# Last half batch of a fused attention / expert / gate kernel: value products over seven steps, copied by ScalarE, no taps in the last four steps

## The chip, the cores and the metric

The kernel runs on one core of a Trainium2 chip. The core has five engines with one instruction queue each, worked off in order: TensorE (PE; its weight loads are shown as PEld), VectorE (DVE), ScalarE (ACT), GpSimd (POOL) and SyncE (SP), which here only issues DMAs. Engines wait for each other by semaphores. The metric is the device time of one execution in microseconds (us), median of three runs.

## The reference, cut to what matters

Three blocks follow each other: attention with pooled queries, a mixture of four experts that are causal attentions of their own, and a gated dense block. The change lies where the second block ends and the third begins.

```python
# second block, per expert e (4 batches of 576 tokens, 512 channels)
scores = scale * (q @ k.transpose(0, 2, 1))      # causal mask, softmax -> a
ye = a @ v @ wo[e]                               # out += weight of e per token * ye
# third block
gate_pre += conv_w[k][None, None, :] * xp[:, k:k + S, :]   # 5 taps along the tokens
gate = 1.0 / (1.0 + np.exp(-gate_pre))
val = x @ w_val
return (gate * val @ w_out)
```

Since `x` is `a @ v @ wo`, the kernel multiplies `wo` and `w_val` together beforehand (the tile `wf`), and computes `val` for a batch straight from the tiles `y` = `a @ v`.

## The kernel before, in words

Everything is computed in fp32 split into a high and a low part (three products for one). The second block walks 40 steps: batch b (4) x half g (2, two experts each) x query tile i (5, in the order 1, 3, 2, 4, 0), plus two trailing steps (LAG = 2). Step n computes scores (`scores2`, L804 or L811, into one of two PSUM buffers `s`; mask and row extreme on DVE, L813 to L816) and their exponentials on ACT (`expo2`, L825 or L827); it normalises the probabilities of step n-1 (`norm2`: three or four small DVE operations, L834 to L844, then a multiplication on POOL, L840 or L845), and transposes those of step n-2 on PE (`transp2`, L864 or L876), from where `evac` (L850) copies them out of PSUM, in turns by ACT and by DVE (both L852/L854). After the last tile of a half, `av2` multiplies probabilities and values on PE (L891, L904); ACT writes the high part of the result (L224), DVE the low part (L225).

Between these fixed parts a step fills PE with work from a list `fill`: it pops entries until the estimated PE time `t` reaches `budget`, which spreads what is in the list over the steps that are `left` until the next half. Behind each popped entry go the DVE and ACT operations that earlier entries left in `late2`, and one "ride": a tap of the convolution on DVE (L215, `tap`), as long as `room` is not used up. So the order on each engine is the order in which this Python code runs; nothing reorders it later.

At step 35 (n = 10 * B - 5), where the last half of the last batch begins, 14 of 16 "value products" of batches 0 and 1 are put into `fill` (`raws`): `value` (L769) makes 6 matmuls of 288 columns into a PSUM tile `a`, and a copy takes it to the tiles called k, q and v in the rows (`first3["raw"]`). The other two follow behind the last `av2`. PSUM tiles named `a` share four banks: a matmul group that takes a bank waits for the last reader of the tile that had it.

Behind the steps comes the third block: sigmoids of the gates (L785), gate times value on DVE (`gate_all`, L1123), eight `mix` groups on PE (L923, with copies L924 and L925 on ACT and their taps on DVE), `spread` (high part on ACT L780, low part on DVE L781) and 18 output groups `final` on PE (L1107), which need these parts and end the kernel.

Of the kernel before, what the change touches and what calls it, by code (L numbers as in the profile page):

```python
# [12 lines left out]
AF = mybir.ActivationFunctionType  # L13
# [7 lines left out]
def tile_kernel(ctx, tc, q, k, v, w_gate, wq, wk, wv, wo, w_val, conv_w, w_out, wo_t, q0, k0, out):  # L21
# [741 lines left out]
    def value(yhs, b, m, hf, then):  # L763

        qsl = slice(hf * HQ, (hf + 1) * HQ)
        ps = ps_m.tile([P, 512], F32, name="a")
        ops = [(wi, yi, g) for g in range(EP) for wi, yi in THREE]
        for o, (wi, yi, g) in enumerate(ops):
            pe.matmul(ps[:, 0:HQ], lhsT=wf[:, g, wi, m * P:(m + 1) * P], rhs=yhs[b, g][:, yi, qsl], start=o == 0, stop=o == len(ops) - 1)  # L769
        late2.append(lambda: then(ps[:, 0:HQ], m, qsl))  # L770
# [16 lines left out]
    with ExitStack() as s2l:  # L787
# [61 lines left out]
        def evac(dst, src):  # L849
            turn[0] += 1  # L850
            if turn[0] % 2:
                act.activation(dst, src, AF.Copy)  # L852
            else:
                dve.tensor_copy(dst, src)  # L854
# [128 lines left out]
        for n in range(len(steps) + LAG):  # L983
            if n < len(steps):
                b, g, i = s = steps[n]
                if n % 5 == 0:
                    pts[b, g] = (pt_p2.tile([P, 4, 2, SQ], F32, name="pt"), pt_p2.tile([R64, 2, R64], F32, name="pt4"))
                    if g == 0 and b:
                        fill += proj(xh[b], 1, (lambda: xh.update({3: load2(3)})) if b == 2 else None)
                        if b == B - 1:  # L990
                            fill.append((0, lambda: late2.append(begin3)))
                    if n == 10 * B - 5:
                        buf = [f(c2.tile([P, 2, SQ], F32R, name=f"k20{i}")) for i in range(2)]
                        bufs = [c2.tile([P, SQ + R64], F32R, name=f"q20{i}") for i in range(2)]
                        v2 = v_p.tile([P, 5, ED + E], F32, name="v2").rearrange("p t c -> p (t c)")
                        first3["raw"] = [[buf[t // 2][:, t % 2] for t in range(KT)], [f(bufs[t])[:, 0:SQ] if t < 2 else v2[:, (t - 2) * SQ:(t - 1) * SQ] for t in range(KT)]]
                        raws = [(0.74, lambda i=i, m=m, hf=hf: value(yhs, i, m, hf, lambda ps, m, qsl: evac(first3["raw"][i][m][:, qsl], ps))) for i in range(2) for m in range(KT) for hf in range(2)]
                        fill += raws[0:14]
                    if b == 0 and g == 1:
                        buf = y0_p.tile([P, EP, 2, SQ], F32R, name="y0")  # L1000
                        yhs.update({(0, i): buf[:, i] for i in range(EP)})
                    if b == 1 and g == 0:
                        buf = y12_p.tile([P, 2, EP, 2, SQ], F32R, name="y12")
                        yhs.update({(1 + j, i): buf[:, j, i] for j in range(2) for i in range(EP)})
                if n % 10 == 5 and b + 1 < B:
                    fill += proj(xh[b + 1], 0)
                if n % 10 == VG and b + 1 < B:
                    v2s[b + 1], gws[b + 1], vg = vgate(xh[b + 1])
                    fill += vg
                if n == 0:  # L1010
                    fill += proj(xh[0], 1)
                if n == FD:
                    fill += [(2.6, lambda g=g: fold(g)) for g in range(EP)]
            t = 0.0
            left = 5 - n % 5
            own = [ahead(m) for m in range(n, n + left)]
            budget = max(FL, (sum(c for c, _ in fill) + (PEND if 10 <= n and n % 10 < PN else 0) + sum(own)) / left) - own[0]

            room = [3]

            def ride():
                if urgent:
                    urgent.pop(0)()
                    return
                if rides and room[0]:
                    room[0] -= 1
                    rides.pop(0)()

            def pop(rider=True):
                c, a = fill.pop(0)  # L1030
                now, late2[:] = late2[:], []
                a()
                for x in now:
                    x()
                if rider:
                    ride()
                return c

            if 0 <= n - 1 < len(steps):
                norm2(steps[n - 1], gws[steps[n - 1][0]])  # L1040
            for _ in range({0: 1, 5: 3}.get(n, 0)):
                t += pop()
            if n < len(steps):
                scores2(s)
            if fill:
                t += pop(RD[n % 5])
            else:
                flush()
            if n >= LAG:
                b1, g1, i1 = steps[n - LAG]  # L1050
                transp2(steps[n - LAG], pts[b1, g1])
                if i1 == ORDER[-1]:
                    if g1 == 1:
                        then = (lambda b1=b1: fill.extend(mix(b1, [yhs[b1, 0], yhs[b1, 1]]))) if b1 < B - 1 else begin_last
                    else:
                        then = (lambda: None) if b1 < B - 1 else load_wo3
                    fill[IN:IN] = av2(v2s[b1], pts[b1, g1], g1, yhs[b1, g1], then)
            if n < len(steps):
                expo2(s)
            if n == 0:  # L1060
                flush()
            while fill and t < budget:
                t += pop()
            ride()
            if n == 9:
                xh[2] = load2(2)
            if n in (12, 22):
                flush()
            if n % 10 == 9:
                flush()  # L1070
                while urgent:
                    urgent.pop(0)()
# [16 lines left out]
    with ExitStack() as s3:  # L1089
# [33 lines left out]
                dve.tensor_tensor(out=raw, in0=raw, in1=first3["gp"][i][m], op=ALU.mult)  # L1123

        gates3 = [(0, lambda i=i, m=m: spread(first3["raw"][i][m], gs[0], m, i * SQ)) for i in range(2) for m in range(KT)]
        rest = values(2, gp2) + values(3, end3["gp"])
        fin = [[(2.6, lambda i=i, t=t: final(i, t)) for t in range(9)] for i in range(2)]
        mixs = mix(B - 1, [yhs[B - 1, g] for g in range(EP)])
# [5 lines left out]
        for i in range(len(VF)):  # L1134
            if i == 9:
                assert len(rest) <= 8
            todo.append((fin[0] + fin[1])[i])
            if i == 0:
                todo.append((0, lambda: gate_all(1)))
                todo += gates3  # L1140
            if i == 2:
                todo.append((0, lambda: sigm(gp2.values())))
            if i == 6:
                todo.append((0, lambda: sigm(end3["gp"].values())))
            todo += rest[0:VF[i]]
            del rest[0:VF[i]]
# [49 lines left out]
```

## Time and profile before

| what | value |
|---|---|
| median of 3 runs | 764.3 us (763.15 to 764.69) |
| the profiled execution, its own time | 763.82 us |
| its span in the trace | 762.0 us |
| PE busy | 746.6 us, 98% of the span |
| DVE busy | 568.6 us, 75% |
| ACT busy | 448.4 us, 59% |
| POOL busy | 316.3 us, 42% |
| mean granted TensorE clock | 0.998 |

The stretch that the change touches lies at 656 to 714 us of the span. A row of the timeline gives the start, the busy time, the engine, the line, the operation, out<-in with shapes and the number of instructions merged into it; in brackets stands how long the engine had been idle and what released it. A busy time includes the emptying of the engine's pipeline, so the next row of the same engine can start before it ends; the cost of an operation in a row without idling is therefore the distance between two starts.

### The profile page before, as it was taken

What the parts mean: (1) busy time and instruction counts of PE and PEld (TensorE: products, weight loads), DVE (VectorE), ACT (ScalarE), POOL (GpSimd) and SP (SyncE); (2) the same over time, 40 slices, a digit from 0 to 9 for tenths busy, and PEclk for the clock granted to TensorE, in tenths of its full rate; (3) what the DMA queues carried; (4) which work ended last, traced back from release to release, by engine and by line L of the source; (5) the groups of instructions that cost most, each with busy time, mean ns of one, the idle gap of its engine ahead of it and who ended that gap; (6) DMA issues with size and microseconds to landing.
All of it is one profiled execution on the core that took longest, in us unless ns stands there. A gap on an engine that the chain in (4) does not pass through costs nothing.

```text
span 762.0 us, 14765 instructions
## 1 busy us (share of the span) xinstructions
PE 746.6 (98%) x5315; PEld 618.1 (81%) x5315; DVE 568.6 (75%) x1062; ACT 448.4 (59%) x986; POOL 316.3 (42%) x443
## 2 busy tenths in 40 slices
PE   8999999999999999999999999999999999989998
PEld 7787887787788777878878877988899888878887
DVE  5777898898888988756766766355789798978730
ACT  5665675665656656656656756335464655647632
POOL 6564675675676675653543511022322322220000
PEclk9999999999999999999999999999999999999999
DMA  6967778778778698777657581478325753800212
GB/s 248 262 144 211 216 198 253 194 227 251 196 243 258 174 269 230 199 210 212 156 166 224 134 281 58 111 210 194 118 64 140 198 145 88 272 1 15 83 57 96
DMA packets 83785, 133.52 MB, mean 175 GB/s; under 512 B 19072, under 2 KB 55424, under 8 KB 83712
## 3 DMA queue, kind: packets, MB, share of 16 engines
q1 hardware_dynamic: 83712, 132.58, 61.2%
q8 instruction: 42, 0.69, 0.4%
q14 instruction: 31, 0.25, 0.1%
HBM read 53.37 MB, written 21.76 MB: 99 GB/s over the span
## 4 chain that ended last, share of the span: by engine, by line
PE 88%; DVE 7%; ACT 2%; DMA 1%; issue 1%; SPq 0%; POOLq 0%; DVEq 0%; ACTq 0%
PE s L440 21%; PE t L489 19%; PE t L519 18%; PE a L242 7%; PE o L1107 7%; PE a L275 4%; PE a L904 3%; PE s L804 2%; PE a L769 2%; DVE gp L215 2%; PE a L876 2%; PE t L478 1%; DVE nm L814 1%; PE a L760 1%; DMA pt<-in_k_dram 1%
## 5 line engine op out<-in xcount | busy, mean ns | idle before, releaser
L452 ACT ACTIVATE p<-s,nm 128x1152 f32<-128x1152 f32 x144 | 176.1, 1223 | 87.1 <-DVE nm L445 84.8
L445 DVE TENSOR_REDUCE nm<-s 128x1 f32<-128x1152 f32 x144 | 192.2, 1352 | 15.6 <-PE s L440 15.3
L489 PE MATMUL t<-ident,p 128*128 128x128 f32 x1296 | 199.0, 275 | 0.8 <-DVE xf L521 0.3
L489 PEld LDWEIGHTS t<-ident,p 128*128 128x128 f32 x1296 | 149.1, 141 | 26.7 <-ACT pt L497 7.0
L497 ACT ACTIVATE pt<-t 128x384 f32<-128x384 f32 x224 | 102.4, 489 | 81.4 <-PE t L489 76.1
L519 PE MATMUL t<-pt,vn 128*64 128x256 f32 (+1 forms) x1152 | 146.8, 408 | 0.0
L499 DVE COPY pt<-t 128x384 f32<-128x384 f32 x208 | 110.3, 554 | 44.8 <-PE t L489 40.9
L519 PEld LDWEIGHTS t<-pt,vn 128*64 128x64 f32 x1152 | 80.1, 137 | 55.8 <-issue 5.3
L440 PE MATMUL s<-ka,qst 128*128 128x384 f32 x384 | 115.8, 383 | 1.7 <-ACT ka L576 1.0
L440 PE MATMUL s<-kb,qst 128*128 128x384 f32 x384 | 99.0, 367 | 0.0
L840 POOL TENSOR_TENSOR p<-p,sm 128x512 f32<-128x512 f32 (+3 forms) x32 | 40.1, 1254 | 106.2 <-DVE sm L838 71.3
L440 PEld LDWEIGHTS s<-kb,qst 128*128 128x128 f32 x384 | 60.8, 189 | 13.6 <-issue 13.1
L440 PEld LDWEIGHTS s<-ka,qst 128*128 128x128 f32 x384 | 63.7, 192 | 3.2 <-ACT ka L576 1.7
L377 POOL TENSOR_TENSOR hlk<-kt,hlk 128x384 fp32r<-128x384 f32 x45 | 45.5, 1011 | 1.1
L521 DVE TENSOR_TENSOR xf<-t,rb 128x320 f32<-128x320 f32 (+1 forms) x32 | 14.6, 457 | 41.4 <-PE t L519 40.8
L242 PE MATMUL a<-xh,wqk 128*128 128x288 f32 x288 | 43.2, 300 | 2.1 <-DVE pt L854 2.1
L825 ACT ACTIVATE p<-s,nm 128x256 f32<-128x256 f32 (+3 forms) x64 | 33.0, 523 | 20.1 <-DVE nm L814 20.1
L467 POOL COPY rm<-rs 128x256 f32<-128x256 f32 x31 | 12.4, 399 | 77.3 <-DVE rs L462 71.2
L528 POOL CAST xt<-xf 128x320 fp32r<-128x320 f32 (+1 forms) x32 | 13.6, 426 | 71.5 <-DVE xf L521 70.9
L215 DVE SCALAR_TENSOR_TENSOR gp<-x,cw,gp 128x572 f32<-128x572 f32 (+3 forms) x48 | 40.7, 850 | 2.6 <-ACT gp L925 2.1
L242 PEld LDWEIGHTS a<-xh,wqk 128*128 128x128 f32 x288 | 39.4, 188 | 3.4 <-DVE pt L854 2.5
L440 PE MATMUL s<-hlk,mixed 128*128 128x384 f32 x135 | 33.7, 357 | 0.0
(190 smaller groups left out, 1170.6 us busy)
## 6 DMA issues: line engine op xcount, KB each, us to landing
ka<-hlk SPq DMA_DIRECT2D x90, 192.0 KB, 3.2
kb<-hlk SPq DMA_DIRECT2D x90, 192.0 KB, 3.6
vn<-in_v_dram SPq DMA_DIRECT2D x16, 576.0 KB, 7.3
k<-hl SPq DMA_DIRECT2D x32, 288.0 KB, 4.9
kt<-in_k_dram SPq DMA_DIRECT2D x15, 576.0 KB, 6.2
qt<-in_q_dram SPq DMA_DIRECT2D x15, 576.0 KB, 5.5
qst<-hlq SPq DMA_DIRECT2D x60, 128.0 KB, 3.3
xh<-x_d SPq DMA_DIRECT2D x12, 576.0 KB, 6.0
```

Of the source, the lines that this page charges most:

```text
L215: dve.scalar_tensor_tensor(out=gp[:, n:], in0=x[:, 0:SQ - n], scalar=cw[:, m, c:c + 1], in1=gp[:, n:], op0=ALU.mult, op1=ALU.add)
L242: pe.matmul(ps[:, 0:HQ], lhsT=wqk[wi][:, t, cs], rhs=xh[t][xi][:, qsl], start=o == 0, stop=o == len(ops) - 1)
L377: late.append(lambda: pool.tensor_tensor(out=hlk[:, 1, gs], in0=kt[:, gs], in1=f(hlk[:, 0, gs]), op=ALU.subtract))
L440: pe.matmul(ps[:, 0:GW], lhsT=ops[c][0], rhs=ops[c][1], start=c == 0, stop=c == len(ops) - 1)
L445: dve.tensor_reduce(d["nm"], d["s"][:, :, 0:GW], axis=AX.XY, op=ALU.min)
L452: act.activation(d["p"], d["s"][:, :, 0:GW], AF.Exp, bias=d["nm"], scale=-1.0, accum_out=sums[(2 * n + u) % len(sums)][:, i:i + 1])
L489: pe.transpose(ps[:, j * P:(j + 1) * P], p[:, g, j * P:(j + 1) * P], ident)
L497: act.activation(dst, src, AF.Copy)
L499: dve.tensor_copy(dst, src)
L519: pe.matmul(ps[64 * h:64 * h + 64, 0:N], lhsT=vn[:, h, j, :], rhs=pt[:, j, h, :], start=j == 0, stop=j == C - 1)
L840: pool.tensor_tensor(out=pv, in0=pv, in1=sm[:, :, None].to_broadcast([P, 2, w]), op=ALU.mult)
L1107: pe.matmul(ps[:, 0:w], lhsT=hl[xi][:, kt, t * P - a:(t + 1) * P - a], rhs=end3["wo3"][:, kt, wi, c:c + w], start=o == 0, stop=o == len(op ...
```

## The change

Three edits, all of them for the last half batch (n >= 35). The copies of the 16 value products are made by ACT alone instead of in turns by ACT and DVE. The budget spreads the list over the steps that are left including the two trailing ones (seven, where it was five), and without the lower bound FL. And `room`, the number of taps that may ride in a step, falls from 3 to 2 at n = 36 and 37 and to 0 from n = 38 on. Two assertions about taps that are left over are added; they make no instruction.

```diff
-                        raws = [(0.74, lambda i=i, m=m, hf=hf: value(yhs, i, m, hf, lambda ps, m, qsl: evac(first3["raw"][i][m][:, qsl], ps))) for i in range(2) for m in range(KT) for hf in range(2)]
+                        raws = [(0.74, lambda i=i, m=m, hf=hf: value(yhs, i, m, hf, lambda ps, m, qsl: act.activation(first3["raw"][i][m][:, qsl], ps, AF.Copy))) for i in range(2) for m in range(KT) for hf in range(2)]
...
-            left = 5 - n % 5
+            left = 5 - n % 5 if n < 35 else len(steps) + LAG - n
             own = [ahead(m) for m in range(n, n + left)]
-            budget = max(FL, (sum(c for c, _ in fill) + (PEND if 10 <= n and n % 10 < PN else 0) + sum(own)) / left) - own[0]
-
-            room = [3]
+            budget = max(FL if n < 35 else 0, (sum(c for c, _ in fill) + (PEND if 10 <= n and n % 10 < PN else 0) + sum(own)) / left) - own[0]
+
+            room = [0 if n > 37 else 2 if n > 35 else 3]
...
+        def check_rides(b):
+            assert not rides if b == B - 1 else len(rides) <= KT * (KC - 1)
+
```

What this does to the order shows at three places. First PE, behind the `av2` of half 0 of the last batch. A name with a number is one tile: `a_...` a PSUM tile of the four banks, `s_...` one of the two score buffers, `p_...` probabilities. Before, the six matmuls of a value product stand between any two fixed parts:

```order
L769 MATMUL a_8715<-y0_6687,wf_6461 128x288 x5
L876 MATMUL a_8730<-ident_62,p_8593 128x128 [waits Activation_49,Pool_49]
L876 MATMUL a_8730<-ident_62,p_8593 128x128 x3
L769 MATMUL a_8738<-y0_6687,wf_6461 128x288 [waits DVE_49,PE_49]
L769 MATMUL a_8738<-y0_6687,wf_6461 128x288 x5
L769 MATMUL a_8747<-y12_7002,wf_6461 128x288 [waits Activation_49]
L769 MATMUL a_8747<-y12_7002,wf_6461 128x288 x5
L811 MATMUL s_8760<-k210_6177,q210_6173 128x288 x2
```

and now, at the same place:

```order
L811 MATMUL s_8712<-k210_6177,q210_6173 128x288 x2
L811 MATMUL s_8712<-k211_6178,q211_6174 128x288 [waits DMAHW5_49,DMAHW0_49]
L811 MATMUL s_8712<-k211_6178,q211_6174 128x288
L811 MATMUL s_8712<-k210_6177,q210_6173 128x288 x2
L811 MATMUL s_8712<-k211_6178,q211_6174 128x288 x2
L769 MATMUL a_8727<-y0_6687,wf_6461 128x288 [waits Activation_49]
L769 MATMUL a_8727<-y0_6687,wf_6461 128x288 x5
L876 MATMUL a_8741<-ident_62,p_8636 128x128 [waits Activation_49,Pool_49]
L876 MATMUL a_8741<-ident_62,p_8636 128x128 x3
L876 MATMUL a_8747<-ident_62,p_8636 128x128 [waits DVE_49]
L876 MATMUL a_8747<-ident_62,p_8636 128x128 x3
L769 MATMUL a_8754<-y0_6687,wf_6461 128x288 [waits DVE_49]
```

In front of these L811 rows PE had made nine value products before and has made four now; the others stand later, up to the second `av2`. The transposes into a_8747 take the bank of a_8681, the first `av2` tile, whose last reader is DVE.

Second DVE at the same place. Before, the low parts of the `av2` result (L225 on hl_8430) stand in front of the small operations of the next step:

```order
L814 TENSOR_REDUCE nm_8706<-s_8705 128x2 [waits DVE_49]
L225 SCALAR_TENSOR_TENSOR hl_8430<-a_8682,hl_8430 128x128 [waits DMAHW2_49,DMAHW1_49,DMAHW7_49,DMAHW0_49,Activation_49]
L225 SCALAR_TENSOR_TENSOR hl_8430<-a_8686,hl_8430 128x448 [waits Activation_49]
L215 SCALAR_TENSOR_TENSOR gp_8559<-x2_8558,cw_97,gp_8559 128x572 [waits DMAHW6_49]
L854 COPY k201_8582<-a_8715 128x288 [waits PE_49]
L215 SCALAR_TENSOR_TENSOR gp_8559<-x2_8558,cw_97,gp_8559 128x573 [waits DVE_49]
L215 SCALAR_TENSOR_TENSOR gp_8559<-x2_8558,cw_97,gp_8559 128x574 [waits DVE_49]
L834 TENSOR_SCALAR sm_8707<-sm_8707 128x2 [waits Activation_49,Pool_49]
```

and now behind them:

```order
L814 TENSOR_REDUCE nm_8672<-s_8671 128x2 [waits DVE_49]
L215 SCALAR_TENSOR_TENSOR gp_8525<-x2_8524,cw_97,gp_8525 128x575
L215 SCALAR_TENSOR_TENSOR gp_8559<-x2_8558,cw_97,gp_8559 128x572 [waits DMAHW6_49]
L834 TENSOR_SCALAR sm_8673<-sm_8673 128x2 [waits Activation_49,Pool_49]
L835 RECIPROCAL sm_8673<-sm_8673 128x2 [waits DVE_49]
L838 TENSOR_TENSOR sm_8673<-sm_8673,gw_7940 128x2 [waits DVE_49]
L813 TENSOR_TENSOR s_8712<-s_8712,cmask2_78 128x64 [waits PE_49]
L814 TENSOR_REDUCE nm_8713<-s_8712 128x2 [waits DVE_49]
L816 TENSOR_TENSOR nm_8713<-nm_8713 128x1 [waits DVE_49]
L225 SCALAR_TENSOR_TENSOR hl_8430<-a_8681,hl_8430 128x128 [waits DMAHW2_49,DMAHW7_49,DMAHW1_49,DMAHW0_49]
L225 SCALAR_TENSOR_TENSOR hl_8430<-a_8685,hl_8430 128x448
```

The low parts moved behind the six operations of sm_8673 and s_8712; the first of these waits for ACT's exponentials p_8674.

Third DVE behind the last `av2`, at the start of the third block. Before:

```order
L225 SCALAR_TENSOR_TENSOR hl_8431<-a_8879,hl_8431 128x448 [waits Activation_49]
L1123 TENSOR_TENSOR k200_8581<-k200_8581,xh_8432 128x576 [waits Activation_49] x2
L1123 TENSOR_TENSOR k201_8582<-k201_8582,xh_8432 128x576 [waits Activation_49] x2
L854 COPY v2_8585<-a_8921 128x288 [waits PE_49]
L781 TENSOR_TENSOR wqk1_8442<-k200_8581,wqk0_8441 128x512 [waits Activation_49]
```

and now:

```order
L225 SCALAR_TENSOR_TENSOR hl_8431<-a_8876,hl_8431 128x448 [waits Activation_49]
L215 SCALAR_TENSOR_TENSOR gp_8559<-x2_8558,cw_97,gp_8559 128x573
L215 SCALAR_TENSOR_TENSOR gp_8559<-x2_8558,cw_97,gp_8559 128x574 [waits DVE_49]
L1123 TENSOR_TENSOR k200_8581<-k200_8581,xh_8432 128x576 [waits Activation_49] x2
L1123 TENSOR_TENSOR k201_8582<-k201_8582,xh_8432 128x576 [waits Activation_49] x2
L215 SCALAR_TENSOR_TENSOR gp_8559<-x2_8558,cw_97,gp_8559 128x575 [waits DVE_49]
L781 TENSOR_TENSOR wqk1_8442<-k200_8581,wqk0_8441 128x512 [waits Activation_49]
```

Three taps that had been done in the steps stand here now, and one copy is gone.

## Rows read from the trace of the kernel before

**Rows 1.** Timeline of PE, last half batch: start us, us, engine, line, operation

```profile
661.15 1.06 PE L769 MATMUL a<-y,wf 128*128 128x288 f32 x6 [1.08 <-DVE pt L854]
...
665.74 0.44 PE L891 MATMUL a<-pt,v 128*64 128x128 f32 x4 [0.80 <-DVE pt L854]
666.01 2.80 PE L904 MATMUL a<-pt,v 128*64 128x448 f32 x20
668.74 0.97 PE L804 MATMUL s<-k,q 128*128 128x384 f32 x4
...
671.51 1.83 PE L769 MATMUL a<-y,wf 128*128 128x288 f32 x12 [0.58 <-DVE hl L225]
673.18 1.22 PE L811 MATMUL s<-k,q 128*128 128x288 f32 x8
674.23 0.96 PE L769 MATMUL a<-y,wf 128*128 128x288 f32 x6
675.03 1.04 PE L876 MATMUL a<-ident,p 128*128 128x128 f32 x8
...
682.42 0.44 PE L876 MATMUL a<-ident,p 128*128 128x128 f32 x2 [0.47 <-POOL p L840]
683.47 0.44 PE L891 MATMUL a<-pt,v 128*64 128x128 f32 x4 [0.61 <-DVE pt L854]
```

**Rows 2.** Timeline of DVE in the same stretch

```profile
661.01 0.45 DVE L854 COPY k<-a 128x288 f32<-128x288 f32 x1
661.38 1.54 DVE L215 SCALAR_TENSOR_TENSOR gp<-x,cw,gp 128x575 f32<-128x575 f32 x2
662.83 0.46 DVE L854 COPY k<-a 128x288 f32<-128x288 f32 x1
663.19 0.16 DVE L834 TENSOR_SCALAR sm<-sm 128x2 f32<-128x2 f32 x1
...
665.27 0.41 DVE L854 COPY pt<-a 128x256 f32<-128x256 f32 x1
...
674.48 0.16 DVE L834 TENSOR_SCALAR sm<-sm 128x2 f32<-128x2 f32 x1
...
676.61 0.45 DVE L854 COPY q<-a 128x288 f32<-128x288 f32 x1
```

**Rows 3.** Timeline of ACT behind the first `av2`

```profile
668.85 0.55 ACT L224 ACTIVATE hl<-a 128x448 fp32r<-128x448 f32 x1 [1.47 <-PE a L904]
671.02 0.60 ACT L852 ACTIVATE pt<-a 128x512 f32<-128x512 f32 x1 [1.62 <-PE a L876]
671.51 0.57 ACT L825 ACTIVATE p<-s,nm 128x384 f32<-128x384 f32 x1
...
672.62 0.42 ACT L852 ACTIVATE k<-a 128x288 f32<-128x288 f32 x1
```

**Rows 4.** Timeline of DVE from the last `av2` to the fifth output group

```profile
687.16 0.62 DVE L225 SCALAR_TENSOR_TENSOR hl<-a,hl 128x448 fp32r<-128x448 f32 x1 [2.61 <-ACT hl L224]
688.58 2.76 DVE L1123 TENSOR_TENSOR k<-k,xh 128x576 f32<-128x576 f32 x4 [0.80 <-ACT xh L785]
...
691.63 0.68 DVE L781 TENSOR_TENSOR wqk<-k,wqk 128x512 fp32r<-128x512 f32 x1
...
712.18 0.42 DVE L781 TENSOR_TENSOR wvg<-v,wvg 128x64 fp32r<-128x64 f32 x2
```

**Rows 5.** Timeline of PE, the fifth output group

```profile
709.52 3.43 PE L1107 MATMUL o<-pt,wvg 128*128 128x512 f32 x12
```

**Rows 6.** Busy time by stretch: length, then PE, PEld, DVE, ACT, POOL, granted clock, DMA

```profile
6.00:9.00 3.00, 1.38 (x5) 0.52 (x4) 1.64 (x2) 1.41 (x4) 0.87 (x1) 1.00 1.04 391
9.00:13.00 4.00, 4.00 (x17) 4.00 (x18) 3.13 (x3) 2.94 (x6) 3.37 (x5) 0.57 1.04 414
...
680.70:684.10 3.40, 2.32 (x20) 1.65 (x20) 1.94 (x7) 1.26 (x6) 0.61 (x1) 1.00 0.00 0
...
696.00:713.00 17.00, 16.98 (x82) 13.64 (x81) 16.79 (x34) 12.24 (x31) 0.00 (x0) 1.00 0.16 62
```

More of the change, by code (lines that the diff above doesn't have):

```diff
@@ L1141, in tile_kernel @@
             if i == 2:
+                todo.append((0, lambda: check_rides(2)))
                 todo.append((0, lambda: sigm(gp2.values())))
             if i == 6:
+                todo.append((0, lambda: check_rides(3)))
                 todo.append((0, lambda: sigm(end3["gp"].values())))
```

## Prediction

> **What bounds the kernel now.** The reading begins with the timeline of PE, since PE is busy nearly all the time and no gap elsewhere can be worth much. In the last half batch the changed stretch, from 656 us to the second `av2` at 683.5, holds its gaps. The four longest are 1.08, 0.80, 0.58 and 0.61 us, and the row behind each names DVE: twice the copy of transposed probabilities, once the low part of the `av2` result, once a copy again [rows 1]. All gaps up to the second `av2` come to about 4 us, with three of 0.25 to 0.5. So 4 us is the most that a better order can bring here. The timeline of DVE shows why PE waits: at 661.0 to 665.7 DVE has no gap, and the copy that PE needs (665.27) is queued behind two value copies, two taps and six operations of the softmax [rows 2]. Then comes the tail. From 696 to 713 both are full, PE 16.98 and DVE 16.79 of 17.00 us [rows 6], and there DVE is the one that decides: the fifth output group takes 3.43 us on PE [rows 5] and ends just behind the last low part that it needs, which DVE begins at 712.18 [rows 4]. Behind that PE runs without a wait to the end. So the end of the kernel moves with DVE's time of arrival at 712, and two things have to be worked out: when the second `av2` comes, and how much more DVE does behind it.
>
> **The copies, part one.** Eight of the 16 copies leave DVE. A copy costs DVE 0.37 us (from 661.01 to 661.38, and 0.36 at the next) [rows 2]; ACT pays about as much, 0.42 us of busy time [rows 3], and has the room. On the path to the first `av2` stand two of them. DVE starts the same taps at 661.0 instead of 661.38, leaves out the second copy, and finishes the probabilities' copy 0.37 + 0.36 = 0.73 earlier, at 664.95 in place of 665.68. The first `av2` needs it, so it starts at 665.0 (665.74 before [rows 1]).
>
> **The spreading.** PE gets there early. Value products are 0.80 us each (674.23 to 675.03 [rows 1]), and only four stand ahead of the first `av2`, where it was six; the scores of the next tile (0.97 us at most) are pulled ahead of it instead. By its own work PE is done at about 663.0: it waits for the copy of the probabilities that ended before 661.15 [rows 1], as before, then does two transposes, one value product and these scores. So it idles 2.0 us where it had idled 0.80. The 0.73 us is gained nevertheless, since DVE sets this time.
>
> **The low part, moved behind a softmax.** The first `av2` takes 3.0 us (665.74 to 668.74 [rows 1]) and ends at 668.05. ACT then makes the high part, one value copy, a copy of four transposed blocks and the exponentials of tile 3. By the distances of [rows 3] that is 0.45 us for the high part, 0.3 for the copy and 0.49 (671.02 to 671.51) for the blocks, so the exponentials begin at 669.35 (PE's transposes are done by then); they take 1.11 us (671.51 to 672.62), and 0.1 until the sum has landed. DVE can start its chain L834 to L816 at 670.6. By then it is through with what the order puts in front (two taps, the chain of tile 3 and its row extremes, two more taps: about 4.8 us from 664.95) and idles. The chain takes 676.61 - 674.48 = 2.13 us [rows 2], and only then comes the low part of `av2`: 672.75 to 673.05. PE meanwhile does four transposes (0.52, half of the row at 675.03), the scores of tile 4 (1.05, 673.18 to 674.23), a value product (0.80) and four more transposes (0.52) [rows 1]: from 668.05 that is 670.95. The next transposes want the bank that DVE has yet to read. So PE idles from 670.95 to 673.1, that is 2.1 us, and this stall takes the place of the one of 0.58.
>
> **From there to the second `av2`.** Nine value products 7.2 us, four and six transposes 0.52 and 0.8, the scores of tile 0 about 0.4 (half of what 384 columns cost is an upper end), five transposes 0.65, and 1.05 from the last transposes to the `av2` (682.42 to 683.47, the wait for the copy included) [rows 1]: 10.6 us. ACT's copies keep ahead of PE here, at 0.3 to 0.42 us each against 0.80 for a product. The narrowest place, by the same walk along the order, is DVE's copy of tile 3's blocks, done about 0.1 us before PE asks for its bank. So the second `av2` starts at 683.7 where it was 683.47: 0.25 us later, though DVE has less to do. If a value product behind a wait costs 0.83 us, as the pair from 671.51 to 673.18 did [rows 1], it is 0.5 later; with a little less ACT time at 669, 0.2 earlier.
>
> **The taps.** `room` 0 leaves three taps of the last channel tile for the tail. DVE runs two of them behind the low part of the second `av2`, in front of the gate products, and the third in the place where the last value copy stood. Before: low part at 687.16, 0.80 us idle, gate products from 688.58, one copy, first low part of `spread` at 691.63 [rows 4]. After: low part at 687.41, taps from 687.95 (0.62 less the overlap), two dependent taps 1.58, so gate products from 689.5 for 2.7, then a tap of 0.73 (half of 661.38 to 662.83 [rows 2]): 692.95. That is 1.3 us later than before, of which 0.25 came with the `av2`; the idle 0.80 us hid part of the three taps. DVE is without a gap from there to 712 [rows 6], so the fifth output group ends 1.3 us later. ACT starts its part of the tail 0.25 + 0.3 later (one more copy), which is less than that and hidden, and PE's eight `mix` groups follow ACT.
>
> **Sum.** -0.73 at the first `av2`, +1.0 in the new wait behind it, +1.05 from the taps: +1.3 us. The profiled execution took 763.8, so 765.1 on its scale; the median of the three runs is 764.3, 0.5 above, so **765.6 us**. Bounds from the places named: second `av2` from 0.2 earlier to 0.5 later, tail 0.8 to 1.4, and 0.3 for the level of a median: 764.7 to 766.6.
>
> **The rivals.** *TensorE's clock falls.* Two gaps of 2 us are longer than any in this stretch so far. The granted clock was 1.00 throughout, also in a stretch in which PE was busy 2.32 of 3.40 us; but at the very start, where PE was busy 1.38 of 3.00 us, the clock of the next 4 us was 0.57, mostly at the lower level of 1.2 GHz [rows 6]. A stretch around either new gap has PE busy for about 1.0 to 1.4 of 3 us, as little as that. One fall costs what the start shows: 0.43 of 4 us, 1.7 us, in matmuls that are on the path (`av2` after the first gap, value products after the second). One gives 767.3, two 769. The Trainium skill (TensorE: Matmul & The Clock Gate, "HAM oscillation — how this bites in real kernels") tells of a clock that falls to half while matmuls wait for transfers, in every turn of a loop, and advises against long idle gaps; its waits are longer than the gaps here, so by its example the clock would hold and the sum would stay at 765.6. The start of this trace speaks against leaning on that: the clock fell there behind waits that were no longer than these.
>
> *DVE's relief pays, not slower.* DVE loses 8 x 0.37 + 3 x 0.73 = 5.2 us of work in a stretch where PE waits for little but DVE. If the exponentials of tile 3 come early enough that the low part is out of the way when PE asks for the bank, the 2.1 us gap goes and the time is 763.5; if the gap before the first `av2` went too, 761.5. It decides itself at the start of DVE's chain L834: it would have to start by 668.5 in place of 670.6. Against it speaks that ACT has the exponentials behind the end of `av2` in its queue.
>
> *The taps are hidden.* If the tail has a wait of DVE's that I don't see, only the 0.25 us stay: 764.6. Against it: 16.79 of 17.00 us [rows 6].
>
> *The edit doesn't do what it says:* it does by the order of instructions, apart from evenness: four products before the first `av2`, ten before the second, four of those in a row.
>
> **How the numbers follow.** A measurement of this kernel can tell about 0.2%, 1.5 us, from no change: 762.8 to 765.8. Forecast 0.42 (0.24 of it below 765.8, 0.18 above); clock 0.27, all slower; DVE's relief 0.2, half of it faster; taps hidden 0.11, no change. So faster 0.10, the same 0.45, slower 0.45. The range reaches into the relief case to 763.0 and over one fall of the clock to 768.0; what is left out is the stronger relief (0.12) and two falls (0.07).
>
> **What would show it.** In the profile of the changed kernel: PE idle for some 2 us ahead of L891 near 665, released by a DVE copy, and for some 2 us near 671 to 673 ahead of L876, released by DVE's L225; DVE idle just before the chain L834 near 670; no PE gap over 0.3 us from there to the second `av2`; three taps around L1123; the output group at 709 stretched by more than the 0.5 us that 3.43 has over its neighbours. Wrong would be: no gap ahead of L876 (the low part comes in time), gaps behind value products that wait for ACT (the copies are late), or a granted clock under 1.00 between 660 and 680.

## The result, and the profile after

The changed kernel takes **769.41 us** (median of six runs, 767.97 to 772.53) against 764.36 (763.15 to 764.69, six runs beside it). The ratio is 1.0070, with a 95% interval of 1.0058 to 1.0082: 5.05 us slower, above the upper end of the forecast range (768.0) and 3.8 us above the forecast.

The mean granted clocks of these six runs lie between 0.991 and 0.998 (before: 0.997 to 1.000); the two runs with 0.998 take 768.6 and 769.1, so the mean clock alone doesn't order the runs.

The profiled execution of after is the slowest of the six: 772.53 us, of which its span is 770.4. Its span is 8.4 us longer than that of before, but 3.5 of these lie ahead of the change: the score group L804 that the changed stretch follows stands at 659.62 and stood at 656.08, and the instructions up to there are the same. So all readings below are distances from that group. Three rows of PE's timeline of before that were not shown yet, the group itself and two output groups (columns: start us, us, engine, line, operation, tiles, shapes, count):

```profile
656.08 0.63 PE L804 MATMUL s<-k,q 128*128 128x256 f32 x4
...
695.98 11.31 PE L1107 MATMUL o<-pt,wqk 128*128 128x512 f32 x48
...
713.58 2.93 PE L1107 MATMUL o<-pt,wvg 128*128 128x512 f32 x12
```

The timeline of PE of after, the rows that answer to these and to [rows 1]:

```profile
659.62 0.63 PE L804 MATMUL s<-k,q 128*128 128x256 f32 x4
...
668.63 0.49 PE L891 MATMUL a<-pt,v 128*64 128x128 f32 x4 [1.94 <-DVE pt L854]
668.88 4.52 PE L904 MATMUL a<-pt,v 128*64 128x448 f32 x20
...
678.83 0.86 PE L876 MATMUL a<-ident,p 128*128 128x128 f32 x4 [2.56 <-DVE hl L225]
679.36 1.81 PE L769 MATMUL a<-y,wf 128*128 128x288 f32 x6
...
690.70 0.44 PE L891 MATMUL a<-pt,v 128*64 128x128 f32 x4 [0.61 <-DVE pt L854]
...
703.51 2.72 PE L1107 MATMUL o<-pt,wqk 128*128 128x512 f32 x11
...
721.86 2.51 PE L1107 MATMUL o<-pt,wvg 128*128 128x512 f32 x10
```

Both gaps of the forecast are there, at the line and with the releaser that it named: 1.94 us ahead of the first `av2`, 2.56 ahead of L876. What the forecast's sum did not have is the length of the work behind them. The same 20 matmuls of L904 take 4.52 us where they took 2.80 [rows 1], and six of L769 take 1.81 where such a group took about 1.0. The granted clock says why. Busy time by stretch of after (length, then PE, PEld, DVE, ACT, POOL, granted clock, DMA share, GB/s):

```profile
614.00:618.00 4.00, 4.00 (x19) 3.95 (x20) 2.75 (x5) 1.59 (x6) 0.00 (x0) 0.57 0.00 1
...
665.00:668.00 3.00, 1.70 (x12) 1.38 (x10) 2.90 (x7) 0.03 (x1) 1.04 (x1) 1.00 0.00 0
...
669.00:672.00 3.00, 3.00 (x12) 1.21 (x10) 2.86 (x8) 1.20 (x5) 1.30 (x1) 0.50 0.00 0
...
675.00:679.00 4.00, 1.44 (x13) 1.20 (x12) 2.50 (x8) 0.90 (x4) 1.47 (x1) 1.00 0.99 335
679.00:682.50 3.50, 3.50 (x17) 3.44 (x17) 2.04 (x8) 1.92 (x5) 0.55 (x1) 0.52 0.53 193
```

Behind each gap the clock is at its lower level, 1.2 GHz: 0.50 from 669 to 672 and, nearly all the time, 0.52 from 679 to 682.5. The prediction had named a clock under 1.00 here as a sign that it would be wrong. In the stretches before, PE was busy 1.70 of 3.00 and 1.44 of 4.00 us. A third fall, at 614 to 618, lies ahead of the change, in work that before has too; it is part of the 3.5 us that this execution brings with it.

The timeline of DVE of after: the wait ahead of the softmax chain, the low part behind it, and the tail that answers to [rows 4].

```profile
676.36 0.17 DVE L834 TENSOR_SCALAR sm<-sm 128x2 f32<-128x2 f32 x1 [2.42 <-ACT p L825]
...
678.50 0.81 DVE L225 SCALAR_TENSOR_TENSOR hl<-a,hl 128x128 fp32r<-128x128 f32 x2
...
694.93 1.66 DVE L215 SCALAR_TENSOR_TENSOR gp<-x,cw,gp 128x573 f32<-128x573 f32 x2
...
699.18 0.81 DVE L215 SCALAR_TENSOR_TENSOR gp<-x,cw,gp 128x575 f32<-128x575 f32 x1
699.91 0.69 DVE L781 TENSOR_TENSOR wqk<-k,wqk 128x512 fp32r<-128x512 f32 x1
```

DVE waits 2.42 us for the exponentials with the low part queued behind the chain, as forecast (the wait is longer than in e9_busy_first below, 0.63, since here the exponentials come behind an `av2` at half clock). The three taps stand in the tail where they were expected.

### The profile page after: what moved, and what is told of

It reads as the page before. It is cut to its first block, busy times and chain, and to the rows that moved or that the text cites. A ratio compares the mean times of both kernels' runs of the same rounds, so it can differ in the third digit from the quotient of the medians.

```text
span 770.4 us, 14766 instructions
## 1 busy us (share of the span) xinstructions
PE 752.7 (98%) x5315; PEld 622.5 (81%) x5315; DVE 566.7 (74%) x1054; ACT 451.0 (59%) x994; POOL 316.9 (41%) x443
## 4 chain that ended last, share of the span: by engine, by line
PE 85%; DVE 8%; DMA 4%; ACT 2%; issue 1%; SPq 0%; DVEq 0%; ACTq 0%
PE s L440 21%; PE t L489 19%; PE t L519 18%; PE a L242 6%; PE o L1107 5%; PE a L275 4%; PE a L904 3%; PE a L769 2%; PE s L804 2%; DVE pt L215 2%; DVE gp L215 1%; PE a L876 1%; DMA k<-hl 1%; PE t L478 1%; DMA xh<-x_d 1%; ACT p L825 1%
## 5 line engine op out<-in xcount | busy, mean ns | idle before, releaser
L224 ACT ACTIVATE hl<-a 128x288 fp32r<-128x288 f32 (+2 forms) x36 | 14.7, 411 | 32.5 <-PE a L242 23.7
```

## The experiments

All kernels have the same instructions up to the score group at 656 us, so one table compares them: for each profiled execution where that group stands, then the distances to the first `av2` (L891), to the second, to the first output group (695.98 in before), to the output group at 713.58 in before, and to the end of the span. "Falls" counts stretches at half clock between that group and the end. The last two columns are over all runs: the median, and the mean of the granted clock (one fall lowers a run's mean by about 0.002; one at the very start, as in [rows 6], counts too, and the profiled execution of before has 0.998 with it).

| kernel | group at | first `av2` | second | output 1 | output 3 | end | sum | falls | median | clock |
|---|---|---|---|---|---|---|---|---|---|---|
| before | 656.08 | 9.66 | 17.74 | 12.51 | 17.60 | 48.4 | 105.9 | 0 | 764.3 | 0.9987 |
| after | 659.62 | 9.01 | 22.06 | 12.81 | 18.35 | 48.5 | 110.8 | 2 | 769.4 | 0.9948 |
| e1_busy | 656.43 | 10.13 | 19.44 | 12.81 | 18.35 | 48.5 | 109.3 | 0 | 768.8 | 0.9973 |
| e2_act_only | 656.37 | 9.25 | 17.03 | 12.81 | 17.58 | 48.5 | 105.2 | 0 | 763.9 | 0.9988 |
| e3_spread_only | 656.38 | 9.28 | 20.98 | 12.51 | 17.60 | 48.5 | 108.8 | 1 | 767.0 | 0.9954 |
| e4_room_only | 655.98 | 9.64 | 17.25 | 12.50 | 19.03 | 48.5 | 106.9 | 0 | 765.7 | 0.9983 |
| e5_low_early | 656.70 | 9.01 | 16.97 | 12.81 | 18.35 | 48.5 | 105.6 | 0 | 765.4 | 0.9978 |
| e6_busy_tight | 657.00 | 8.93 | 19.11 | 12.82 | 18.35 | 48.5 | 107.7 | 0 | 766.8 | 0.9997 |
| e7_act_but_last | 657.35 | 9.26 | 17.02 | 12.51 | 17.59 | 48.5 | 104.9 | 0 | 763.8 | 0.9991 |
| e8_mended | 656.30 | 8.92 | 18.84 | 12.51 | 17.61 | 48.5 | 106.3 | 0 | 764.8 | 0.9990 |
| e9_busy_first | 656.94 | 8.94 | 20.50 | 12.81 | 18.37 | 48.5 | 109.1 | 1 | 767.5 | 0.9980 |
| e10_no_room | 657.48 | 9.02 | 20.33 | 12.81 | 17.60 | 48.5 | 108.3 | 1 | 768.3 | 0.9952 |
| e11_low_first | 655.95 | 9.26 | 16.53 | 12.52 | 17.61 | 48.5 | 104.4 | 0 | 762.6 | 0.9992 |
| e12_low_tap | 657.97 | 8.53 | 16.53 | 12.50 | 17.60 | 48.5 | 103.7 | 0 | 762.2 | 0.9983 |

The theory to test: the change costs a little by its order and tail, and the rest is TensorE's clock, which falls behind two PE gaps that part two makes. The rival: the order costs it all, and the clock is only an onlooker.

**e1_busy: something to do in the gaps.** Matmuls of the identity with itself go into a bank that is overwritten next, 14 ahead of the first `av2` and 14 ahead of the transposes of L876.

```
+ if then is load_wo3:
+     for _ in range(14):
+         pe.matmul(box[0][:, 0:P], lhsT=ident, rhs=ident, start=True, stop=True)
...
+ if s == (B - 1, 1, 3) and e0 == 0:
+     for _ in range(14):
+         pe.matmul(ps[:, 0:P], lhsT=ident, rhs=ident, start=True, stop=True)
```

> The changed kernel with 14 matmuls of 128 columns that nobody reads put into each of the two places where TensorE sits idle for about 2 us (into the first av2 tile ahead of L891, and into the bank of tile 3's first transposes ahead of L876). They keep TensorE at work while it would wait, and lengthen no wait that counts by more than 0.3 us. Theory A (the order costs 1.3 us, and each idle time of about 2 us lets the granted clock fall, at 1.7 us a fall): no fall at 1.2 GHz between 655 us and the second av2, time 765.5 to 766.5. Theory B (the clock is beside the point, the new waits themselves or a later start of the last stretch cost the 5 us): time stays at 769 to 770.

768.81 us (767.06 to 770.02), ratio 1.0059 (1.0042 to 1.0077): by the number, close to theory B. The trace tells another story. No stretch behind the gaps is at half clock, and yet the way from the group to the end is 3.4 us longer than before. The timeline of PE of e1_busy:

```profile
663.35 3.29 PE L894 MATMUL a<-ident 128*128 128x128 f32 x28
666.56 0.44 PE L897 MATMUL a<-pt,v 128*64 128x128 f32 x4
```

The 14 matmuls take 3.29 us, more than the gap that they fill, and delay the first `av2` to 10.13 us behind the group, where after has 9.01; the expectation had allowed for 0.3. Three of the six runs have a mean clock of 0.995 or 0.996 and take 769.8 to 770.0, three have 0.998 or 1.0 and take 767.1 to 767.8. The experiment added a cost of its own and could not decide; e6 mends it.

**e2, e3, e4: the three parts alone.** e2_act_only has part one, the copies on ScalarE:

```
- evac(first3["raw"][i][m][:, qsl], ps)
+ act.activation(first3["raw"][i][m][:, qsl], ps, AF.Copy)
```

> The kernel before with the first edit alone: the 16 value copies on ScalarE, order of PE as before, five steps, room 3. Theory A: the waits of TensorE for VectorE shrink (the 0.80 us ahead of the first av2 by two copies of 0.37 us), the tail on VectorE is one copy shorter, no long idle time, no fall of the clock: 762.5 to 764.0. Theory B (ScalarE's queue is what is late): 765 or more.

763.92 us (762.38 to 765.14), ratio 0.9995 (0.9985 to 1.0004). In the profile the second `av2` comes 1.1 us earlier, of which 0.30 is lost ahead of the first output group and some 0.35 outside the span (last section). The median alone is not told apart from before.

e3_spread_only has part two, the spreading:

```
- left = 5 - n % 5
+ left = 5 - n % 5 if n < 35 else len(steps) + LAG - n
...
- budget = max(FL, (sum(c for c, _ in fill) + (PEND if 10 <= n and n % 10 < PN else 0) + sum(own)) / left) - own[0]
+ budget = max(FL if n < 35 else 0, (sum(c for c, _ in fill) + (PEND if 10 <= n and n % 10 < PN else 0) + sum(own)) / left) - own[0]
```

> The kernel before with the second edit alone: budget over seven steps without the lower bound, copies in turns, room 3. Theory A: the two idle times of about 2 us are made by this edit, so it has them without the others, VectorE is even later ahead of the first av2 (two copies more), and the clock falls once or twice: 766.5 to 770. Theory B (spreading is harmless, the copies or the taps cost the time): 763.5 to 765.

766.98 us (765.73 to 770.74), ratio 1.0038 (1.0023 to 1.0054): the part that costs. PE of e3_spread_only:

```profile
665.66 0.44 PE L891 MATMUL a<-pt,v 128*64 128x128 f32 x4 [2.21 <-DVE pt L854]
665.93 4.23 PE L904 MATMUL a<-pt,v 128*64 128x448 f32 x20
...
675.23 0.66 PE L876 MATMUL a<-ident,p 128*128 128x128 f32 x4 [2.04 <-DVE hl L225]
...
681.03 1.06 PE L769 MATMUL a<-y,wf 128*128 128x288 f32 x6 [0.68 <-DVE pt L854]
```

The two gaps belong to part two; the third, 0.68, is one that part one takes away, since there a DVE copy stands in the queue. Behind the gap of 2.21 the clock fell (L904 takes 4.23), behind that of 2.04 it did not, though PE was no busier around it than in the stretches of after that lost the clock, 1.19 of 3.00 us:

```profile
672.00:675.00 3.00, 1.19 (x10) 0.95 (x8) 2.10 (x7) 0.66 (x4) 1.47 (x1) 1.00 0.97 349
675.00:679.00 4.00, 3.77 (x30) 3.66 (x31) 3.96 (x8) 1.87 (x5) 0.00 (x0) 1.00 0.61 228
```

So a gap of 2 us can bring a fall and need not.

e4_room_only has part three, fewer taps in the last steps:

```
- room = [3]
+ room = [0 if n > 37 else 2 if n > 35 else 3]
```

> The kernel before with the third edit alone: taps in the last steps fewer, the rest of them in the tail. Theory A: VectorE's part behind the second av2 is about 1.4 us longer (three taps of 0.73 less the 0.80 us of idle time), the waits before it are up to 1 us shorter, no idle time near 2 us, no fall of the clock: 764.4 to 765.8. Theory B (the taps cost most of the 5 us): 768 or more.

765.71 us (764.23 to 766.78), ratio 1.0018 (1.0008 to 1.0027), as expected of the taps. Without part two PE gains 0.5 us up to the second `av2` and then stands for the low parts in the tail, PE of e4_room_only:

```profile
699.16 8.86 PE L1107 MATMUL o<-pt,wqk 128*128 128x512 f32 x37 [1.06 <-DVE wqk L781]
```

**e6_busy_tight: the same with sized fillings**, 8 matmuls in the first gap and 10 in the second (the diff of e1_busy with `range(8)` and `range(10)`).

> The whole change, with matmuls that nobody reads in PE's two gaps, as in e1_busy but sized to the gaps: 8 ahead of the first av2 and 10 ahead of L876, at 0.235 us each by e1_busy (3.29 us for 14), 1.9 and 2.35 us. Theory (the time of the change is an order cost of about 0.9 at the second av2 and 1.05 in the tail, and the rest is clock): 764.3 + 1.95 = 766.3, within 765.9 to 766.9, and a mean clock of 0.998 or more. Rival (the clock has little part in it, and the 768.8 of e1_busy is the order): 767.8 to 769.

766.83 us (765.00 to 768.14, 7 runs), ratio 1.0032 (1.0019 to 1.0045); six of the seven runs have a mean clock of 1.000, the seventh 0.998. The timeline of PE, and the stretches of e6_busy_tight that answer to those of after:

```profile
663.92 1.95 PE L894 MATMUL a<-ident 128*128 128x128 f32 x16
665.93 0.44 PE L897 MATMUL a<-pt,v 128*64 128x128 f32 x4
666.20 2.80 PE L910 MATMUL a<-pt,v 128*64 128x448 f32 x20
...
671.28 2.39 PE L876 MATMUL a<-ident 128*128 128x128 f32 x20
...
674.43 0.66 PE L879 MATMUL a<-ident,p 128*128 128x128 f32 x4 [0.33 <-DVE hl L225]
...
685.03 0.44 PE L897 MATMUL a<-pt,v 128*64 128x128 f32 x4 [0.61 <-DVE pt L854]
```

```profile
669.00:672.00 3.00, 3.00 (x25) 3.00 (x26) 2.37 (x4) 2.46 (x7) 0.99 (x1) 1.00 0.62 167
672.00:675.00 3.00, 2.67 (x24) 2.33 (x23) 2.86 (x9) 0.00 (x0) 1.47 (x1) 1.00 0.90 300
675.00:679.00 4.00, 4.00 (x31) 3.85 (x31) 2.45 (x8) 2.97 (x10) 1.15 (x1) 1.00 0.48 178
```

Adding work that nobody needs makes the kernel 2.6 us faster than after, and L904 takes its 2.80 us again. The waits themselves have not gone, only what PE does meanwhile. So the clock is the cause of 2.6 of the 5.1 us by the medians (2.95 between the two `av2` of the profiled executions, 22.06 against 19.11), and the rival falls. Of the rest, the order costs 107.7 - 105.9 = 1.8 us in the span at full clock, and 0.35 lies outside the span (last section); the 0.3 that remain are within the intervals.

**e9_busy_first: the filling in the first gap only** (8 matmuls ahead of the first `av2`).

> The whole change with 8 idle matmuls in the first gap only (as in e6_busy_tight, which has them in both). Theory (each gap brings its own clock fall, about 1.4 us): the fall behind the second gap stays, 766.8 + 1.4 = 768.2, within 767.5 to 768.9, and the mean clock is 0.998, one fall, in most runs. Rival (the first gap alone brings the clock down, the second one only because it follows): 766.8 and a mean clock of 1.0.

767.47 us (766.26 to 768.86, 6 runs), ratio 1.0040 (1.0027 to 1.0054), against e6 by the medians 0.6 us, in the profiled execution 1.4. The median lies just below the theory's range and 0.7 above the rival, and the intervals of e9 and e6 overlap; so the trace has to decide. PE and the stretches of e9_busy_first:

```profile
674.37 0.66 PE L876 MATMUL a<-ident,p 128*128 128x128 f32 x4 [2.55 <-DVE hl L225]
```

```profile
672.00:675.00 3.00, 0.63 (x5) 0.52 (x5) 2.86 (x9) 0.00 (x0) 1.47 (x1) 1.00 1.05 386
675.00:679.00 4.00, 4.00 (x21) 3.98 (x21) 1.93 (x7) 1.92 (x5) 1.15 (x1) 0.58 0.34 124
```

The second gap brings its own fall without one at the first, and the distance between the two `av2` is 20.50 against 19.11 in e6: 1.4 us for one fall. In after, with both, it is 22.06: another 1.6 (the L904 behind the first gap alone is 1.7 longer, 4.52 against 2.80). It does not happen in each run: two of the six have a mean clock of 1.000, and they are the two fastest (766.26 and 766.46); the other four take 767.1 to 768.9.

**e5_low_early: the low part ahead of the chain.** The two low-part instructions of the first `av2` go out before the chain of tile 4.

```
+ if n == 38:
+     flush()
  if 0 <= n - 1 < len(steps):
      norm2(steps[n - 1], gws[steps[n - 1][0]])
```

> The whole change, but the low part of the first av2 (two instructions, L225) is issued ahead of the softmax chain of tile 4 (L834 to L816) and not behind it. Theory (the second gap is the place of L225 in DVE's queue): the gap of 2.56 us ahead of L876 falls below 0.3 us, with it the 2.3 us of order and the clock fall of about 1.4 us behind it; the first gap with its fall stays. 769.4 - 2.3 - 1.4 = 765.7, within 765.0 to 766.5. Rival (PE would wait there for the probabilities of the next tile anyway, so the gap moves to the next transposes): 768.0 to 769.5, a gap of 2 us at the six transposes.

765.44 us (763.14 to 767.52, 11 runs), ratio 1.0014 (1.0004 to 1.0025): the theory's 765.7. PE and DVE of e5_low_early:

```profile
665.71 0.44 PE L891 MATMUL a<-pt,v 128*64 128x128 f32 x4 [1.95 <-DVE pt L854]
...
671.06 1.03 PE L876 MATMUL a<-ident,p 128*128 128x128 f32 x8
...
674.61 1.08 PE L876 MATMUL a<-ident,p 128*128 128x128 f32 x6 [0.49 <-DVE pt L854]
```

```profile
670.93 0.81 DVE L225 SCALAR_TENSOR_TENSOR hl<-a,hl 128x128 fp32r<-128x128 f32 x2
671.66 0.15 DVE L834 TENSOR_SCALAR sm<-sm 128x2 f32<-128x2 f32 x1
```

The eight transposes run in one piece, the gap of 2.56 is gone, and one of 0.49 is all that is late next. Four us of the 5.1, the fall behind the second gap included, hung on the place of two instructions in DVE's queue. Here, too, the gap of 1.95 was followed by no fall in the profiled execution, while three of the eleven runs have a mean clock of 0.996, which before never has; this suggests a fall in those.

It also settles a false trail. The chain of waits of after does not name DVE's chain ahead of L225 but a load of weights (a chain's columns: start us, us, what):

```profile
673.63 4.82 DMA pt<-w_d
678.45 0.05 issue
678.50 0.29 DVE hl L225
```

That load did move: part two makes it wait for the first `av2` (issued at 673.21, at 654.15 in before), which the prediction had not seen. But in e5 it is issued at 668.60 and lands some 6 us later, while L225 starts at 670.93. So L225 doesn't wait for it; that it landed just before L225 in after is a coincidence. Its reader, the first output group, comes some 20 us later.

**e10_no_room: parts one and two, the taps as before** (`room = [3]`).

> Parts one and two without part three (three taps may ride in each step, so none is left for the tail). Theory (part three costs its taps in the tail, 1.05 us, and gives back the 0.5 us that taps take between the two av2): 769.4 - 1.05 + 0.5 = 768.8, within 768.2 to 769.3, with both gaps and both falls. Rival (the parts add up as they do alone: -0.4 for part one, +2.7 for part two): 766.6.

768.27 us (766.11 to 770.08, 6 runs), ratio 1.0050 (1.0034 to 1.0065): the 768.8 of the theory is within the interval, the 766.6 of adding up the parts just outside. Since the 766.6 has the intervals of e2 and e3 in it, this doesn't refute adding up. In the profile the tail is 0.75 us shorter than in after (17.60 against 18.35), which is the taps. Both gaps are there, 1.94 and 2.56, but only the second was followed by a fall. The 0.5 us that the theory gave back doesn't show: between the two `av2` it is 20.33 here and 20.50 in e9, which has one fall too and fewer taps there. That parts one and two together cost 3.9 us by the medians, where they cost -0.4 and 2.7 alone, stays open: from the group at 656 to the end e10 is 0.5 us shorter than e3, with one fall in each and about the same mean clock, and the intervals of the two overlap.

**e7, e8, e11, e12: towards a better version.** e7 is part one, but the last two copies stay as they were, one of them on DVE (it also has e5's two lines, which leave DVE's order as it is in e2). e8 is parts one and two with the low part early, 8 filling matmuls in the first gap, and the last copies as in e7. e11 is e7 with the low part behind DVE's chain of tile 3 and ahead of its mask, e12 is e11 with one tap moved from ahead of the first `av2` into DVE's idle time behind it.

```
- act.activation(first3["raw"][i][m][:, qsl], ps, AF.Copy)
+ evac(first3["raw"][i][m][:, qsl], ps) if (i, m) == (1, KT - 1) else act.activation(first3["raw"][i][m][:, qsl], ps, AF.Copy)
```

The line above is in all four. The rest of e12 follows; e11 has of it only `if n == 37:` and `flush()`.

```
  if 0 <= n - 1 < len(steps):
      norm2(steps[n - 1], gws[steps[n - 1][0]])
+ if n == 37:
+     ride()
+     flush()
...
- room = [3]
+ room = [{35: 2, 37: 4}.get(n, 3)]
...
- t += pop(RD[n % 5])
+ t += pop(RD[n % 5] and n != 35)
```

> Part one alone, with the last two copies left as they were (one on ScalarE, one on DVE). In the profile of part one alone the second av2 came 0.81 us earlier than before by the distance from the group at 656, and 0.3 of it was lost between that av2 and the first output group. Theory (the 0.3 is ScalarE's extra copy there): 764.3 - 0.8 = 763.5, within 763.1 to 763.9. Rival (the 0.3 is something else): 763.9, as with part one alone.

763.79 us (762.27 to 764.83, 11 runs), ratio 0.9992 (0.9983 to 1.0000). Between the two expectations in the median, but the trace shows the 0.30 back: second `av2` to first output group 12.51 in place of 12.81, with one copy less on ScalarE. The 0.8 of the expectation is what was left at the first output group; the second `av2` itself is 1.1 earlier in e2 and in e7, of which the median shows 0.5.

> Parts one and two with three mendings: the low part of the first av2 ahead of the softmax chain, 8 idle matmuls in the first gap that hold the clock, the last copy on DVE; and the taps as before (none left for the tail). Theory (the order of part two is good once its two gaps are mended): second av2 0.8 to 1.3 us earlier than before by the distance from the group at 656, the tail as before: 763.0 to 763.6. Rival (with the taps in, DVE makes PE wait at another place between the two av2): 764.3 to 765.5.

764.78 us (763.80 to 766.35, 11 runs), ratio 1.0012 (1.0003 to 1.0021): the rival. PE of e8_mended has new waits between the two `av2`, and ScalarE, which releases the first of them, has waited for DVE itself:

```profile
673.56 0.74 ACT L827 ACTIVATE p<-s,nm 128x576 f32<-128x576 f32 x1 [1.32 <-DVE nm L816]
```

```profile
674.84 0.85 PE L876 MATMUL a<-ident,p 128*128 128x128 f32 x6 [1.14 <-ACT k L1000]
...
678.43 1.07 PE L769 MATMUL a<-y,wf 128*128 128x288 f32 x6 [1.11 <-DVE pt L854]
```

With the taps kept out of the tail, DVE makes PE wait in the middle: 18.84 between the `av2` against 16.97 in e5, which has the taps in the tail. So with the low part early, part three buys time there; with the low part late it doesn't, as e10 shows. e8 has the filling matmuls besides, which end ahead of this stretch.

> e7_act_but_last with the low part of the first av2 one place earlier on DVE: behind the chain of tile 3 (L834 to L838) and ahead of its mask and row extremes, where DVE idled 1.26 us in the profile of part one alone. Theory (the gap of 0.57 ahead of the value products goes): 763.8 - 0.5 = 763.3, within 762.8 to 763.6. Rival (the row extremes come 0.35 later, and with them the exponentials and the next gap): 763.8.

762.64 us (762.18 to 764.06, 11 runs), ratio 0.9982 (0.9973 to 0.9990): better than expected. The distance between the `av2` falls by 0.49, which is the gap (0.58 in e7). The median falls by 1.15; where the rest comes from isn't shown, and the intervals of e7 and e11 overlap.

> e11_low_first, and one tap of DVE is moved from ahead of the first av2 to behind it, into the same idle 1.26 us; the copy of tile 4's transposed block goes ahead of the tap in front of it. Theory (the two gaps ahead of the first av2, 1.07 and 0.40 us, are DVE's work there): first av2 0.73 earlier, 763.3 - 0.73 = 762.6, within 762.1 to 763.1. Rival (the tap and the low part together outgrow the idle time, and the exponentials of tile 3 come late): 763.3 to 764.

**762.17 us** (760.88 to 763.80, 10 runs), ratio 0.9973 (0.9964 to 0.9982): faster than both kernels, by 2.2 us (0.3%) than before. PE of e12_low_tap:

```profile
662.30 1.06 PE L769 MATMUL a<-y,wf 128*128 128x288 f32 x6 [0.35 <-DVE pt L854]
```

The gap that was 1.08 in before [rows 1] is 0.35, and the first `av2` stands 8.53 behind the group against 9.26 in e11: the 0.73 of one tap. The median gains only 0.5 of it, for a reason outside the span (last section).

## Why the prediction was wrong, step by step

**The first `av2`, 0.73 earlier: right.** 9.66 - 8.93 = 0.73 in e6. The gap ahead of it, forecast 2.0, is 1.94.

**The second gap: right in place and cause, 0.4 short.** Forecast 2.1, measured 2.55 in e9, where the first `av2` runs at full clock. The step that is off is the landing of the exponentials' sum, put at 0.1 us: DVE's chain starts 0.46 us behind ScalarE's last row (last section). The rest was as worked out: PE is done with its own work 5.94 us behind the start of the first `av2` in e9, forecast 5.95, and from that gap to the second `av2` 685.03 - 674.43 = 10.60 in e6, forecast 10.6.

**The tail, 1.05: right in sum, wrong in its parts.** 12.82 + 18.35 - 12.51 - 17.60 = 1.06 in e6. But 0.30 of it is ScalarE's one copy more, which the prediction called hidden: it alone gives 12.81 in e2, and e7 without it 12.51. PE's last `mix` groups wait for ScalarE (0.29 and 0.30 us in after, released by L925), so the first output group moves with it, as this row of ScalarE of after shows, the copy between the four sigmoids and the first copy of `mix`:

```profile
697.40 0.40 ACT L997 ACTIVATE v<-a 128x288 f32<-128x288 f32 x1
```

The taps are the other 0.75 (18.35 against 17.60 in e10). In e4, where ScalarE has no copy more, they cost 1.4.

**The sum at full clock: 1.3 forecast, 1.8 measured** in the span of e6 (-0.73 at the first `av2`, +1.37 up to the second, +1.06 in the tail, 0.1 behind it), and 0.35 outside it that no row of before could have told.

**TensorE's clock: here it failed.** The prediction had the mechanism as a rival, with its place, the rows for it and its price: two falls, 769 us. The median is 769.4, and a fall measures 1.4 to 1.7 us where 1.7 were put. What failed is the weight: the sum put the clock at nothing, where e6 shows it to be worth 2.6 us; the rival had a chance of 0.27, and two falls, at 0.07, were left out of the range. The rows said more than that. [rows 6] has one stretch behind which the clock fell, with PE busy 1.38 of 3.00 us, and one behind which it held, 2.32 of 3.40; for the stretches around the new gaps the prediction itself worked out 1.0 to 1.4 of 3, on the side of the first. After has 1.70 of 3.00 and 1.44 of 4.00, and lost the clock behind both. A higher chance was due, but no certainty: e3 kept the clock behind 1.19 of 3.00.

The prediction weighed against it the Trainium skill (TensorE: Matmul & The Clock Gate, "HAM oscillation — how this bites in real kernels"), whose waits are longer than these, and by which the time would be 765.6. The runs disagree: gaps of 1.94 and 2.56 us were enough. The next section of the same page of the Trainium skill, "A second HAM failure mode: psum-queue depth-cycling", tells of a clock lost to short idle times between groups of matmuls that go round the PSUM banks. The second gap is a wait for such a bank, the first one for probabilities; so that section speaks for one fall, which at the prediction's price gives 767.3, and it names no price itself.

**The other rivals.** DVE's relief brings the second `av2` 1.1 us earlier in e2 and 1.4 in e5, where the low part is early; the time falls clear of noise only in e11 and e12. The taps were not hidden. The edit did what it says.

## What to carry to other kernels

A gap of 2 us on TensorE at full clock may cost nearly twice its length, so when an order is changed, price each new gap with a fall behind it too, from a stretch of the same trace in which the clock fell. How busy the engine is around the gap warns of it but doesn't decide it (e3); a filling sized to the gap tells what is clock and what is order (e6). Spreading work evenly over steps is not the same as filling waits: the even order took products away from the places where PE waits for DVE. What a stalled engine waits for is often one short instruction queued behind a long wait of another's; moving that one brought the most here, 4.0 us by the medians in e5 and 1.15 in e11.

## What the runs showed of the hardware that was not expected

**Time outside the span.** The time of a run less its span is 1.73 to 1.86 us in every run of before, e3, e4, e7, e8 and e11, and 2.10 to 2.28 in every run of after, e1, e2, e5, e6, e9, e10 and e12. The 0.35 us between the two groups belong to the program, not to the run, and no record within the span shows them. Which property decides is open: it is not the number of copies on ScalarE, since e11 and e12 have the same.

**The landing of a sum.** In e9_busy_first the last row of the exponentials on ScalarE and the first of the chain that waits for them on DVE, and the same pair in e3_spread_only:

```profile
671.21 0.23 ACT L825 ACTIVATION_READ_ACCUMULATOR p<-s,nm 128x1 f32 x1
```

```profile
671.90 0.17 DVE L834 TENSOR_SCALAR sm<-sm 128x2 f32<-128x2 f32 x1 [0.63 <-ACT p L825]
```

```profile
672.45 0.21 ACT L825 ACTIVATION_READ_ACCUMULATOR p<-s,nm 128x1 f32 x1
```

```profile
672.76 0.17 DVE L834 TENSOR_SCALAR sm<-sm 128x2 f32<-128x2 f32 x1 [1.70 <-ACT p L825]
```

From the end of the one to the start of the other it is 0.46 us in e9 and 0.10 in e3. It is 0.45 or 0.46 at this place in after, e1, e6, e9 and e10, and 0.02 to 0.11 in all other waits of this chain for ScalarE in these traces. That ScalarE idles behind the sum is not the reason: it does so for 3.6 us in e9 and for 3.3 in e3. The cause stays open.

**The clock's chance.** Of gaps of about 2 us, those of 1.94 and 2.56 in after, 2.21 in e3, 2.55 in e9 and 2.56 in e10 were followed by a fall, those of 2.04 in e3, 1.95 in e5 and 1.94 in e10 were not. The gap of 1.94 stands ahead of the same `av2` in after and in e10, so one profiled execution shows what can happen and the mean clock over the runs how often.
